# A fused attention and two-MoE kernel: the first block's output matmul in plain fp32, its weights split later, and a planner with other durations and due times

## The chip, the cores and the metric

The kernel runs on one core of a Trainium2 chip. The metric is the device time of one execution in microseconds. The core has a matrix engine (TensorE, PE in the rows), three engines for elementwise work (VectorE or DVE, ScalarE or ACT, GpSimd or POOL), and DMA queues, which SyncE (SP) issues. Each engine takes its instructions strictly in the order in which they were written; what couples the engines are semaphores.

## The reference

Three stages, each on the result of the one before, all float32:

```python
# attention: linear attention with decay, in chunks; x is [4, 8, 768, 32], B and C [4, 8, 768, 16]
    L = np.exp(cum[:, :, :, None] - cum[:, :, None, :]) * causal
    y = einsum(CB * L, xc) + einsum(Cc, state) * exp(cum)
    state = decay_full * state + sum(Bx)
# first MoE: 3072 tokens, d_model 256, d_ff 1536
    xn = x / rms * rms_g
    g = xn @ w_gate
    silu = g * (1.0 / (1.0 + np.exp(-g)))
    return silu * (xn @ w_val) @ w_out
# second MoE: d_ff 1024
    h = x @ w_in
    solu = h * softmax(h)
    return layernorm(solu) * g_ln @ w_out
```

## The kernel before

The 3072 tokens are 24 units of 128, in six blocks of four units. A unit goes through attention (`lpe`, `cb`, `mt`, `y`, `ms`, `rb`, `xn`, `xh`, `xl`: one matmul group for the decays and products, one for the result `y`, then the normalisation, which writes the split input of the first MoE). A block of 512 tokens goes through the first MoE in 12 steps of 128 hidden columns: a gate matmul group `g_gate` (six matmuls into `pg`), a value group `g_val` (six into `pv`), the activation (`g_tanh` on ACT, `g_silu` and `g_mul` on DVE), and the output `o_mm` (two halves, `po0` and `po1`, three matmuls each). Then a unit goes through the second MoE: `m_h` (12 matmuls into `ph`), the softmax on DVE and ACT, a transpose through DRAM (`m_tr`, `m_ds`, `m_dl`, tiles `dt`, `scr`, `tt`), a split of the result into `uth` and `utl` (`m_thd` on ACT, `m_tld` on DVE), and `m_f` (24 matmuls into `pf`). The last four units take a transpose on PE instead.

A float32 product at the fast rate needs split operands: a value is kept as a high part in the reduced type float32r and a low part, the difference, and a product is high x high, low x high and high x low, so three matmuls. The high part is a copy on ACT (`w_hi` for weights, `g_ah` for the activation), the low part a subtraction on DVE or GpSimd (`w_lo`, `g_al`). The weights of the MoEs come in as float64 bits of which DVE makes float32 in three instructions a piece (`w_conv`, lines 114, 117 and 120; 26 pieces of 512 columns: gate, value and output weights of the first MoE in turn, then those of the second). They are converted while the first two blocks run.

The order on every engine is made by a planner in the kernel (`plan`, line 994): `op(name, engine, duration, due, ...)` lists the operations with what they come after, which buffers they take (`new`) and use, and the planner places them one by one, at each engine the one with the earliest due time among those that could start soonest. Durations and due times only set the order; on the chip the semaphores decide. `alt` lets DVE work go to GpSimd. Due times come from constants: `PRO`, `FIRST` and `per1, perA, per2` give the start of each block, `Y0`, `YPOS`, `YSPAN` the attention, `HLAG` and `TAILGAP` the second MoE, `WGAP` and `wdue` the weights.

In what follows block, step and unit count from 0: unit 14's `ph` is the fifteenth group of 12 matmuls on line 473, its `pf` the fifteenth group of 24 on line 602.

Of the kernel before, what the change touches and what calls it, by code (L numbers as in the profile page):

```python
# [26 lines left out]
LAG = 2  # L27
AHEAD = 4
PRO = 34.0
FIRST = 63.0  # L30
WARM = 7
Y0 = (9.0, 4.0)
YPOS, YSPAN = 0.65, 1.0
TAILGAP = 5.0
SLACK = 0.1
SLACK0 = 0.1
VALATE = 5.0
EARLY = (-1.0, 1.5, 4.0, 6.0)
NPE = 4
MARGIN = {"PE": 0.5}  # L40
CROW = 30.0
WGAP = 8.0
HLAG = (50.0, 26.0)
# [3 lines left out]
        "xts": 2, "s2": 2, "ob": 1, "dt": 1, "scr": 2}  # L47
# [3 lines left out]
def fused_kernel(ctx, tc, aT, xbt, bcT, wg, wv, wo1, rg, wi2, wo2, gl, consts, out):  # L51
# [46 lines left out]
    wo2_s = wt([8, DM], "wo2")  # L98
# [24 lines left out]
    def w_f32(i):  # L123
        return wtm[i].bitcast(F32).rearrange("p (k f) -> p k f", k=2)
# [54 lines left out]
    def p_hi(c):  # L179
        A.activation(wo2_s[0][:, 4 * c:4 * c + 4], w2[c], AF.Copy)  # L180
# [434 lines left out]

    def g_mm(b, f, ws, tag):
# [87 lines left out]
    per1, perA, per2 = 12.4, 2.7, 6.5  # L704
# [44 lines left out]
    for u in range(NU):  # L749
        b, k = unit_blk[u]  # L750
        n = blk[b][1]
        if b == 0:
            Y = Y0[0] + Y0[1] * k
        else:
            Y = start[b - 1] + (k + YPOS) * (start[b] - start[b - 1]) / n * YSPAN
        s0 = u % 6 == 0
        if u >= SPLIT:
            op(f"lbc{u}", "SP", 1.6, Y - 14, (ld_bc4, u), new=[("bc", f"bc{u}")], kb=700)
# [44 lines left out]
        if u >= SPLIT:  # L803
            op(f"cb{u}", "PE", 0.5, Y - 12.0, (at_cbr, u), after=cbok + Lok[1], new=[("hc", f"pcb{u}")],
# [5 lines left out]
        op(f"y{u}", "PE", (1.4 if not s0 else 1.1) + (1.05 if yc else 0.0), Y, (at_ycb if yc else at_y, u),  # L810
# [24 lines left out]
    for b in range(NB):  # L835
# [3 lines left out]
        for f in range(NF):  # L839
# [12 lines left out]
            op(f"mu{s}", "DVE", v_us(N), t, (g_mul, b, f), after=[f"si{s}", f"vm{s}"], use=[f"th{s}", f"pv{s}"])  # L852
# [5 lines left out]
            for m in range(2):  # L858
                op(f"o{m}{s}", "PE", mm_us(N, 3), to, (o_mm, b, f, m), after=[f"al{s}"] + wo_n + ([f"o{m}{b}.{f-1}"] if f else []) + ([f"o0{s}"] if m else []),
# [18 lines left out]
    for u in range(NU):  # L878
# [12 lines left out]
        if not tl:  # L891
            op(f"h{u}.1", "PE", mm_us(512, 12), H, (m_h2, u), after=x2ok + win, new=[("hc", f"ph{u}")],
# [101 lines left out]
    def plan():  # L994
# [48 lines left out]
        while len(order) < len(ops):  # L1043
# [20 lines left out]
            if e != o["e"]:  # L1064
                o = ops[nm] = dict(o, us=o["alt"][0], fn=o["alt"][1])
# [116 lines left out]
```

## Time and profile before

| | us |
|---|---|
| Median of 3 runs | 558.02 (557.35 to 560.51) |
| The profiled execution | 554.45 |
| Its span, first to last instruction | 552.6 |
| PE busy | 524.9 (95%) |
| DVE busy | 422.8 (77%) |
| ACT busy | 309.5 (56%) |
| GpSimd busy | 117.7 (21%) |

The profile has the time of each instruction, what ended the idle time ahead of it, and the clock that PE was granted, as a share of 2.4 GHz. A busy time is the union of an engine's instructions; matmuls overlap each other in the pipeline, so that PE can be busy all the time and still not be at its peak. The rows of PE show an fp32 matmul as two records. "Critical" in the headings below is the chain of work that ended last, followed back from the last instruction.

### The profile page before, as it was taken

To read this page: it belongs to the slowest core of one execution; us is meant where nothing else is said; L and a number is where in the kernel's file an instruction comes from. 1 tells how busy PE (TensorE), PEld (TensorE's weight loads), DVE (VectorE), ACT (ScalarE), POOL (GpSimd) and SP (SyncE) were. 2 spreads that over 40 slices of the span, in tenths; PEclk is the share of its full clock that TensorE was granted. 3 is DMA by queue.
4 is the path that set the end of the run, shared out by engine and by line. 5 is a ranking of instruction groups with operands and counts; after the bars stand their busy time and mean duration, and the time that the engine had idled before them with its cause. 6 is when DMAs were issued, how large, how long until landed. Compare 5 with 4: busy or idle time off the path is not lost.

```text
span 552.6 us, 9279 instructions
## 1 busy us (share of the span) xinstructions
PE 524.9 (95%) x3240; PEld 438.2 (79%) x3240; DVE 422.8 (77%) x802; ACT 309.5 (56%) x670; POOL 117.7 (21%) x140
## 2 busy tenths in 40 slices
PE   8869998999999999999999999999999799999886
PEld 8847876777788888888888878878888688887786
DVE  4887999999996898778887878877875565375674
ACT  6526655565675675566674665765643343344455
POOL 1522443550320120424112212013302000010000
PEclk9868999999999999999999999999999899999999
DMA  5664755561174252363353264242221221022200
GB/s 169 182 194 148 232 186 187 180 191 57 46 219 144 86 178 91 105 185 108 104 167 105 80 184 134 92 148 93 56 86 49 77 79 55 11 76 87 85 21 28
DMA packets 44014, 65.00 MB, mean 118 GB/s; under 512 B 7360, under 2 KB 30272, under 8 KB 43968
## 3 DMA queue, kind: packets, MB, share of 16 engines
q1 hardware_dynamic: 43968, 64.42, 37.2%
q8 instruction: 25, 0.41, 0.3%
q14 instruction: 21, 0.17, 0.1%
HBM read 50.57 MB, written 13.83 MB: 117 GB/s over the span
## 4 chain that ended last, share of the span: by engine, by line
PE 64%; DVE 20%; DMA 7%; issue 4%; ACT 3%; SPq 2%; POOL 0%; DVEq 0%; ACTq 0%; POOLq 0%
PE pv L622 12%; PE pg L622 12%; PE po L664 11%; PE pf L602 11%; PE ph L473 10%; DMA xb<-in_xbt_dram 3%; DVE wt L117 3%; DVE wt L120 2%; DMA tt<-scr 2%; DVE th L644 2%; DVE th L640 2%; DVE al L656 2%; PE y L363 2%; DVE utl L578 2%; PE y L358 1%
## 5 line engine op out<-in xcount | busy, mean ns | idle before, releaser
L650 ACT ACTIVATE ah<-th 128x512 fp32r<-128x512 f32 x72 | 45.3, 629 | 61.9 <-PE po L664 38.2
L656 DVE TENSOR_TENSOR al<-th,ah 128x512 fp32r<-128x512 f32 x61 | 45.2, 740 | 25.7 <-ACT ah L650 25.4
L640 DVE SCALAR_TENSOR_TENSOR th<-th,pg 128x512 f32<-128x512 f32 x72 | 49.2, 684 | 18.5 <-ACT th L636 17.9
L622 PE MATMUL pg<-xh,wg_h 128*128 128x512 f32 x144 | 60.7, 421 | 2.7 <-DVE th L640 1.3
L664 PE MATMUL po<-ah,wo_h 128*128 128x512 f32 x144 | 58.9, 409 | 0.0
L664 PE MATMUL po<-al,wo_h 128*128 128x512 f32 x144 | 56.7, 393 | 2.2 <-DVE al L656 2.2
L622 PE MATMUL pv<-xh,wv_h 128*128 128x512 f32 x144 | 58.4, 406 | 0.2 <-DVE th L644 0.2
L622 PE MATMUL pg<-xl,wg_h 128*128 128x512 f32 x144 | 57.4, 399 | 0.4 <-DVE xl L442 0.4
L622 PE MATMUL pg<-xh,wg_l 128*128 128x512 f32 x144 | 57.0, 396 | 0.0
L622 PE MATMUL pv<-xl,wv_h 128*128 128x512 f32 x144 | 56.8, 394 | 0.0
L622 PE MATMUL pv<-xh,wv_l 128*128 128x512 f32 x144 | 56.8, 394 | 0.0
L664 PE MATMUL po<-ah,wo_l 128*128 128x512 f32 x144 | 56.7, 394 | 0.0
L602 PE MATMUL pf<-wo_h,utl 128*128 128x256 f32 x176 | 50.8, 289 | 5.4 <-DVE utl L578 5.4
L644 DVE TENSOR_TENSOR th<-pv,th 128x512 f32<-128x512 f32 x72 | 49.7, 690 | 7.0 <-PE pv L622 1.2
L602 PE MATMUL pf<-wo_h,uth 128*128 128x256 f32 x176 | 50.3, 286 | 4.1 <-ACT uth L573 4.1
L227 ACT ACTIVATE L<-L,cneg 128x128 f32<-128x128 f32 x160 | 50.5, 390 | 5.3 <-DMA L<-crow 5.1
L636 ACT ACTIVATE th<-pg 128x512 f32<-128x512 f32 x72 | 42.6, 592 | 17.8 <-PE pg L622 17.3
L602 PE MATMUL pf<-wo_l,uth 128*128 128x256 f32 x176 | 50.2, 285 | 0.0
L538 POOL TENSOR_TENSOR sc<-sc,mhalf 128x1 f32<-128x1 f32 x24 | 13.5, 564 | 169.3 <-DVE sc L533 165.2
L602 PEld LDWEIGHTS pf<-wo_h,utl 128*128 128x128 f32 x176 | 34.4, 195 | 7.4 <-DVE utl L578 6.7
L602 PEld LDWEIGHTS pf<-wo_h,uth 128*128 128x128 f32 x176 | 33.9, 192 | 5.7 <-ACT uth L573 5.0
L473 PE MATMUL ph<-wi_h,xh 128*128 128x512 f32 x96 | 37.9, 395 | 0.2 <-DVE L L298 0.2
(151 smaller groups left out, 1225.8 us busy)
## 6 DMA issues: line engine op xcount, KB each, us to landing
L<-crow SPq DMA_DIRECT2D x20, 512.0 KB
scr<-dt SPq DMA_DIRECT2D x20, 512.0 KB
tt<-scr SPq DMA_DIRECT2D x80, 128.0 KB
bc<-in_bcT_dram SPq DMA_DIRECT2D x48, 128.0 KB
stage<-in_wo_dram SPq DMA_DIRECT2D x10, 512.0 KB
xb<-in_xbt_dram SPq DMA_DIRECT2D x24, 192.0 KB
stage<-in_wg_dram SPq DMA_DIRECT2D x6, 512.0 KB
stage<-in_wv_dram SPq DMA_DIRECT2D x6, 512.0 KB
```

The costliest lines, as they stand in the source:

```text
L117: V.scalar_tensor_tensor(out=t, in0=v[:, :, 1], scalar=-0x40000000, in1=t, op0=ALU.bitwise_and, op1=ALU.bitwise_or)
L227: A.activation(d["L"][:, h], d["L"][:, h], AF.Exp, bias=cneg[:, u * 8 + h:u * 8 + h + 1])
L473: T.matmul(ph[c], xx[:, kk, k * P:(k + 1) * P], ww[:, kk, 512 * c:512 * c + 512], start=(i == 0), stop=(i == 5))
L538: G.tensor_tensor(out=sc[:, 7:8], in0=sc[:, 6:7], in1=mhalf, op=ALU.pow)
L602: T.matmul(d["pf"][:, 0:DM], uu[:, k], ww[:, k], start=(k == 0 and i == 0), stop=(k == 7 and i == 2))
L622: T.matmul(ps[:, :n], ww[:, kk, f * P:(f + 1) * P], xx[:, kk, :n], start=(i == 0), stop=(i == 5))
L636: A.activation(d["th"], d["pg"], AF.Tanh, scale=0.5)
L640: V.scalar_tensor_tensor(out=d["th"], in0=d["th"], scalar=1.0, in1=d["pg"], op0=ALU.add, op1=ALU.mult)
L644: V.tensor_tensor(out=d["th"], in0=d["pv"], in1=d["th"], op=ALU.mult)
L650: A.activation(d["ah"], d["th"], AF.Copy)
L656: e.tensor_tensor(out=d["al"], in0=d["th"], in1=d["ah"].bitcast(F32), op=ALU.subtract)
L664: T.matmul(po[b, m][:, :n], ww[:, f, m * P:(m + 1) * P], aa, start=(f == 0 and i == 0), stop=(f == NF - 1 and i == 2))
```

## The change

In block 0 the output matmul takes its operands unsplit, one plain fp32 matmul for each half of a step. `g_mul` writes its result into a buffer `aw`, in the storage of `ah` and `al` by turns, and `o_mm` multiplies it with the raw float32 weights, which the last conversion instruction now writes into a buffer `wraw` of their own (in the storage that the second MoE's `wo2` takes later). `g_ah` and `g_al` fall away in block 0. The split of the output weights, `w_hi` and `w_lo`, gets a due time 8 us ahead of block 1's use, and `w_lo` comes after the fp32 matmuls on the same piece. Besides, the planner's constants and durations have new values, and each block's attention and second MoE get an offset of their own (`YO`, `HO`).

```diff
-PRO = 34.0
-FIRST = 63.0
+PRO = 39.6
+FIRST = 61.0
...
-HLAG = (50.0, 26.0)
+HLAG = (52.3, 20.9)
+YO = (2.4, 2.27, 0.0, 2.59, -2.9)
+HO = (9.9, 2.75, 0.0, 0.0, -10.0, -6.6)
...
+    def w_raw(i):
+        c = pieces[i][0][1]
+        while len(wraw) <= c // 4:
+            nm = f"wo2_{'hl'[len(wraw)]}"
+            wraw.append(wp.tile([P, 4, 512], I32, name="wraw", tag=nm, bufs=1))
+        return wraw[c // 4][:, c % 4]
...
-            V.scalar_tensor_tensor(out=t, in0=v[:, :, 0], scalar=29, in1=t, op0=ALU.logical_shift_right,
+            raw = w_raw(i) if pieces[i][0][0] == "o" else t
+            V.scalar_tensor_tensor(out=raw, in0=v[:, :, 0], scalar=29, in1=t, op0=ALU.logical_shift_right,
                                    op1=ALU.bitwise_or)
...
     def g_mul(b, f):
         d = act[b, f]
-        V.tensor_tensor(out=d["th"], in0=d["pv"], in1=d["th"], op=ALU.mult)
+        out = d["th"]
+        if b < WIDE:
+            out = d["aw"] = sp.tile([P, NMAX], F32, name="aw", tag=awtag(f), bufs=BUFS[awtag(f)])[:, :blk[b][1] * P]
+        V.tensor_tensor(out=out, in0=d["pv"], in1=d["th"], op=ALU.mult)
...
-        for i, (aa, ww) in enumerate(((d["ah"], wo1_s[0]), (d["al"], wo1_s[0]), (d["ah"], wo1_s[1]))):
+        if b < WIDE:
+            T.matmul(po[b, m][:, :n], w_raw(3 * (f // 2) + 2).bitcast(F32)[:, 256 * (f % 2) + m * P:256 * (f % 2) + (m + 1) * P], d["aw"], start=f == 0,
+                     stop=f == NF - 1)
+        for i, (aa, ww) in enumerate(() if b < WIDE else ((d["ah"], wo1_s[0]), (d["al"], wo1_s[0]), (d["ah"], wo1_s[1]))):
...
-        op(f"wl{i}", "SP", 0.45, EARLY[i] if i < len(EARLY) else t - 6, (w_load, i), after=[f"wl{i-1}"] if i else [], new=[("u", f"st{i}")], kb=512)
+        op(f"wl{i}", "SP", 0.45, EARLY[i] if i < len(EARLY) else t - LEAD, (w_load, i), after=[f"wl{i-1}"] if i else [], new=[("u", f"st{i}")], kb=512)
...
+        if kind == "o":
+            t = gdue(WIDE, 2 * c + LAG) - 8.0
+            wu = [f"raw{c // 4}"]
...
+            last = [f"o{m}{b}.{2 * c + q}" for b in range(WIDE) for q in range(2) for m in range(2)]
...
-        op(f"w{i}", "DVE", 0.68, t, (w_lo, i, V), after=[f"wh{i}"], use=[f"wt{i}"], lock=True)
+        op(f"w{i}", "DVE", 0.68, t, (w_lo, i, V), after=[f"wh{i}"] + last, use=wu, lock=True)
...
+        H += HO[b]
```

`LEAD` is -2.11, and `WIDE` is 1.

What the change makes of the order is seen best at three places. The first is DVE in block 0, at step 0. Before, from the conversion of the second piece of gate weights (`L114` to `L120` into `wt`), with the activation of step 0 (`L640`, `L644`) and the low part `al`:

```order
L114 TENSOR_SCALAR wt<-stage 128x512
L640 SCALAR_TENSOR_TENSOR th<-th,pg 128x512
L644 TENSOR_TENSOR th<-pv,th 128x512
L117 SCALAR_TENSOR_TENSOR wt<-stage,wt 128x512
L120 SCALAR_TENSOR_TENSOR wt<-stage,wt 128x512
L656 TENSOR_TENSOR al<-th,ah 128x512
```

Now, at the same step (`L662` and `L669` are the activation, `L128` to `L135` the conversion):

```order
L135 SCALAR_TENSOR_TENSOR wraw<-stage,wt 128x512
L662 SCALAR_TENSOR_TENSOR th<-th,pg 128x512
L669 TENSOR_TENSOR aw<-pv,th 128x512
L128 TENSOR_SCALAR wt<-stage 128x512
L131 SCALAR_TENSOR_TENSOR wt<-stage,wt 128x512
L135 SCALAR_TENSOR_TENSOR wt<-stage,wt 128x512
```

The low part is gone, and the conversion of an output weight piece, into `wraw`, now ends right ahead of the activation of step 0.

The second place is PE at the passage from block 4 to block 5, where unit 14's `pf` begins. Before, ahead of it stand the last transpose of the attention (`y`) and the last output step of block 4 (two halves):

```order
L420 MATMUL y<-ident,r 128x128
L664 MATMUL po_4132<-ah,wo_h 128x512
L664 MATMUL po_4132<-al,wo_h 128x512
L664 MATMUL po_4132<-ah,wo_l 128x512
L664 MATMUL po_4144<-ah,wo_h 128x512
L664 MATMUL po_4144<-al,wo_h 128x512
L664 MATMUL po_4144<-ah,wo_l 128x512
L602 MATMUL pf<-wo_h,uth 128x256
L602 MATMUL pf<-wo_h,utl 128x256
L602 MATMUL pf<-wo_l,uth 128x256
```

Now, ahead of it stands the gate matmul of block 5, step 1:

```order
L644 MATMUL pg<-xh,wg_h 128x512
L644 MATMUL pg<-xl,wg_h 128x512
L644 MATMUL pg<-xh,wg_l 128x512
L621 MATMUL pf<-wo_h,uth 128x256
L621 MATMUL pf<-wo_h,utl 128x256
L621 MATMUL pf<-wo_l,uth 128x256
```

The same `pf` has moved behind the end of block 4's `ph` groups and into block 5. From unit 14's `ph` to it, PE's order has, now, the output step 7 of block 4, gate and value of step 10, output steps 8 and 9, gate and value of step 11, unit 15's `ph`, gate and value of block 5's step 0, output step 10 and that gate.

The third place is PE behind the last output matmul of block 5. Before:

```order
L664 MATMUL po_4918<-ah,wo_h 128x512
L664 MATMUL po_4918<-al,wo_h 128x512
L664 MATMUL po_4918<-ah,wo_l 128x512
L602 MATMUL pf<-wo_h,uth 128x256
L602 MATMUL pf<-wo_h,utl 128x256
L602 MATMUL pf<-wo_l,uth 128x256
```

Now:

```order
L692 MATMUL po_4856<-ah,wo_h 128x512
L692 MATMUL po_4856<-al,wo_h 128x512
L692 MATMUL po_4856<-ah,wo_l 128x512
L492 MATMUL ph<-wi_h,xh 128x512
L492 MATMUL ph<-wi_h,xl 128x512
L492 MATMUL ph<-wi_l,xh 128x512
```

Unit 18's `pf` stood there and unit 20's `ph` stands there now; unit 18's `pf` has moved ahead of the last gate matmul. The last output step is now behind two others (steps 9, 10 and 11 in a row), and behind it come the `ph` of units 20 and 21, then unit 19's `pf`.

## Rows read from the trace of the kernel before

**Rows 1.** Windows, by stage: stretch, length, engines' busy time (instructions), clock, DMA share, GB/s.

```profile
38.20:107.00 68.80, 65.55 (x411) 51.36 (x411) 62.69 (x116) 39.52 (x99) 25.21 (x26) 0.96 0.60 190
107.00:185.10 78.10, 75.45 (x467) 61.25 (x467) 70.88 (x126) 48.64 (x110) 20.76 (x23) 1.00 0.41 129
185.10:432.00 246.90, 245.82 (x1494) 206.28 (x1493) 189.98 (x358) 148.42 (x311) 52.08 (x59) 1.00 0.37 117
432.00:441.00 9.00, 5.89 (x30) 5.18 (x29) 6.58 (x14) 4.74 (x9) 0.55 (x1) 0.81 0.15 59
...
509.40:552.60 43.20, 33.39 (x227) 29.91 (x225) 25.71 (x68) 22.59 (x46) 2.71 (x5) 1.00 0.13 43
```

**Rows 2.** Critical chain, block 2: start, duration, engine and line, count.

```profile
243.87 1.39 PE pg L622 x6
```

**Rows 3.** Timeline of PE, start of the program: start, duration, instruction.

```profile
7.55 0.49 PE L978 MATMUL pd<-la,um 128*128 128x192 f32 x2
7.88 1.05 PE L269 MATMUL po<-um,la 128*128 128x128 f32 x8
8.86 1.16 PE L291 MATMUL pcb<-bc 16*128 16x128 f32 x16
```

**Rows 4.** Groups by line and shape, block 0: count, busy, mean ns, idle before.

```profile
L622 PE MATMUL pg<-xh,wg_h 128*128 128x512 f32 x25 | 11.3, 451 | 2.0 <-ACT xh L438 1.2 <-DVE th L640 0.8
...
L664 PE MATMUL po<-al,wo_h 128*128 128x512 f32 x22 | 8.7, 397 | 2.2 <-DVE al L656 2.2
...
L656 DVE TENSOR_TENSOR al<-th,ah 128x512 fp32r<-128x512 f32 x10 | 7.1, 712 | 0.3 <-ACT ah L650 0.3
```

**Rows 5.** Timeline in block 0, where PE waits for a low part.

```profile
94.44 1.59 DVE L120 SCALAR_TENSOR_TENSOR wt<-stage,wt 128x512 int32<-128x512 int32 x1
...
96.94 0.50 PE L664 MATMUL po<-al,wo_h 128*128 128x512 f32 x1 [2.24 <-DVE al L656]
```

**Rows 6.** Timeline ahead of block 0: DVE, a conversion and unit 2's state.

```profile
27.24 1.00 DVE L120 SCALAR_TENSOR_TENSOR wt<-stage,wt 128x512 int32<-128x512 int32 x1
...
28.68 0.27 DVE L379 SCALAR_TENSOR_TENSOR s<-s,e,y 128x64 f32<-128x64 f32 x1
```

**Rows 7.** Critical chain: `ph` and `pf` of unit 6, `ph` of units 14 and 18.

```profile
251.37 2.72 PE ph L473 x12
...
272.88 2.82 PE pf L602 x24
...
417.47 2.75 PE ph L473 x12
...
493.44 2.72 PE ph L473 x12
```

**Rows 8.** Timeline of the passage from block 4 to block 5.

```profile
432.44 0.40 PE L664 MATMUL po<-ah,wo_l 128*128 128x512 f32 x1
...
433.91 1.22 DVE L507 SCALAR_TENSOR_TENSOR ut<-ph,ut 128x1024 f32<-128x1024 f32 x1 [0.20 <-ACT ut L497]
...
434.88 0.38 PE L602 MATMUL pf<-wo_h,uth 128*128 128x256 f32 x1 [2.03 <-ACT uth L573]
...
435.06 1.22 DVE L578 TENSOR_TENSOR utl<-tt,uth 128x1024 fp32r<-128x1024 f32 x1
...
436.33 0.38 PE L602 MATMUL pf<-wo_h,utl 128*128 128x256 f32 x1 [1.08 <-DVE utl L578]
```

**Rows 9.** Timeline of the tail.

```profile
509.40 0.60 ACT L673 ACTIVATE xh<-po 128x512 fp32r<-128x512 f32 x1 [4.17 <-PE po L664]
...
512.16 0.38 PE L602 MATMUL pf<-wo_h,uth 128*128 128x256 f32 x1 [2.10 <-ACT uth L573]
...
513.62 0.38 PE L602 MATMUL pf<-wo_h,utl 128*128 128x256 f32 x1 [1.08 <-DVE utl L578]
...
527.23 0.39 PE L602 MATMUL pf<-wo_h,utl 128*128 128x256 f32 x1 [2.34 <-DVE utl L578]
```

**Rows 10.** Critical chain, the first load of weights.

```profile
2.18 5.49 DMA stage<-in_wg_dram
```

More of the change, by code (lines that the diff above doesn't have):

```diff
@@ L27 @@
 LAG = 2
+LEAD = -2.11
+PER = (12.7, 1.3, 6.5)
+WIDE = 1
 AHEAD = 4
-PRO = 34.0
-FIRST = 63.0
+PRO = 39.6
+FIRST = 61.0
 WARM = 7
[L32 to L36, printed above, removed]
+Y0 = (12.7, 2.9)
+YPOS = 0.58
+YSPAN = 0.84
+TAILGAP = 8.9
+SLACK = 0.19
+SLACK0 = 0.18
 VALATE = 5.0
-EARLY = (-1.0, 1.5, 4.0, 6.0)
+EARLY = (-1.0, -2.46, 4.0, 6.0)
 NPE = 4
 MARGIN = {"PE": 0.5}
-CROW = 30.0
-WGAP = 8.0
-HLAG = (50.0, 26.0)
+CROW = 37.3
+WGAP = 11.0
+HLAG = (52.3, 20.9)
+YO = (2.4, 2.27, 0.0, 2.59, -2.9)
+HO = (9.9, 2.75, 0.0, 0.0, -10.0, -6.6)
 TRACE = None
@@ L179, in p_hi @@
     def p_hi(c):
+        if not wo2_s:
+            wo2_s.extend(wp.tile([P, 8, DM], F32R, name=f"wo2_{s}", bufs=1) for s in "hl")
         A.activation(wo2_s[0][:, 4 * c:4 * c + 4], w2[c], AF.Copy)
@@ L731, in fused_kernel @@
             continue
-        op(f"wh{i}", "ACT", 0.63, t, (w_hi, i), after=[f"wc{i}.2"], use=[f"wt{i}"])
-        op(f"w{i}", "DVE", 0.68, t, (w_lo, i, V), after=[f"wh{i}"], use=[f"wt{i}"], lock=True)
+        wu = [f"wt{i}"]
+        last = []
+        if kind == "o":
+            t = gdue(WIDE, 2 * c + LAG) - 8.0
+            wu = [f"raw{c // 4}"]
+            ops[f"wc{i}.2"]["new"] += [(f"wo2_{'hl'[c // 4]}", wu[0])] if c % 4 == 0 else []
+            ops[f"wc{i}.2"]["use"] += wu
+            last = [f"o{m}{b}.{2 * c + q}" for b in range(WIDE) for q in range(2) for m in range(2)]
+        op(f"wh{i}", "ACT", 0.63, t, (w_hi, i), after=[f"wc{i}.2"], use=wu)
+        op(f"w{i}", "DVE", 0.68, t, (w_lo, i, V), after=[f"wh{i}"] + last, use=wu, lock=True)
         alt(f"w{i}", p_us(512), (w_lo, i, G))
@@ L740, in fused_kernel @@
         op(f"psub{c}", "DVE", 1.22, t, (p_sub, c), after=["pmean"], use=["mean"], lock=True)
-        op(f"phi{c}", "ACT", 1.06, t, (p_hi, c), after=[f"psub{c}"], use=["w2h", "w2l"])
+        op(f"phi{c}", "ACT", 1.06, t, (p_hi, c), after=[f"psub{c}"], use=["w2h", "w2l"],
+           new=[] if c else [("wo2_h", "w2H"), ("wo2_l", "w2L")])
         op(f"plo{c}", "DVE", 1.22, t, (p_lo, c), after=[f"phi{c}"], use=["w2h", "w2l"], lock=True)
@@ L803, in fused_kernel @@
         if u >= SPLIT:
-            op(f"cb{u}", "PE", 0.5, Y - 12.0, (at_cbr, u), after=cbok + Lok[1], new=[("hc", f"pcb{u}")],
+            op(f"cb{u}", "PE", 0.48, Y - 12.0, (at_cbr, u), after=cbok + Lok[1], new=[("hc", f"pcb{u}")],
                use=[f"bh{u}", f"cb{u}", f"pcb{u}"])
@@ L851, in fused_kernel @@
             op(f"si{s}", "DVE", v_us(N), t, (g_silu, b, f), after=[f"th{s}"], use=[f"th{s}", f"pg{s}"])
-            op(f"mu{s}", "DVE", v_us(N), t, (g_mul, b, f), after=[f"si{s}", f"vm{s}"], use=[f"th{s}", f"pv{s}"])
+            wide = b < WIDE
+            op(f"mu{s}", "DVE", v_us(N), t, (g_mul, b, f), after=[f"si{s}", f"vm{s}"], new=[(awtag(f), f"aw{s}")] if wide else [],
+               use=[f"th{s}", f"pv{s}"] + ([f"aw{s}"] if wide else []))
+            for m in range(2) if wide else ():
+                op(f"o{m}{s}", "PE", mm_us(N, 4), to, (o_mm, b, f, m), after=[f"mu{s}", f"wc{3*(f//2)+2}.2"] + ([f"o{m}{b}.{f-1}"] if f else []) + ([f"o0{s}"] if m else []),
+                   new=[(f"po{m}", f"po{m}{b}")] if f == 0 else [], use=[f"aw{s}", f"po{m}{b}", f"raw{f // 8}"])
+            if wide:
+                continue
             op(f"ah{s}", "ACT", a_us(N, 0.02), t + 2, (g_ah, b, f), after=[f"mu{s}"], new=[("ah", f"ah{s}")],
@@ L891, in fused_kernel @@
         if not tl:
-            op(f"h{u}.1", "PE", mm_us(512, 12), H, (m_h2, u), after=x2ok + win, new=[("hc", f"ph{u}")],
+            op(f"h{u}.1", "PE", mm_us(512, 12) + 0.02, H, (m_h2, u), after=x2ok + win, new=[("hc", f"ph{u}")],
                use=[f"ph{u}", f"x2{b}"])
@@ L940, in fused_kernel @@
         if not tl:
-            op(f"f{u}.3", "PE", mm_us(DM, 24), H + 1, (m_f4, u), after=[f"tl{u}.1"] + wout, new=[(tt[0], f"pf{u}")],
+            op(f"f{u}.3", "PE", 24 * 0.118, H + 1, (m_f4, u), after=[f"tl{u}.1"] + wout, new=[(tt[0], f"pf{u}")],
                use=[f"pf{u}"] + ku)
         for c in range(4) if tl else ():
-            op(f"f{u}.{c}", "PE", mm_us(DM, 6), H + 1, (m_f, u, c), after=[f"tl{u}.{c//2}"] + (wout if c == 0 else [f"f{u}.{c-1}"]),
+            op(f"f{u}.{c}", "PE", 6 * 0.118, H + 1, (m_f, u, c), after=[f"tl{u}.{c//2}"] + (wout if c == 0 else [f"f{u}.{c-1}"]),
                new=[(tt[0], f"pf{u}")] if c == 0 else [], use=[f"pf{u}"] + ku)
-        op(f"out{u}", "ACT", 0.4, H + 2, (m_out, u), after=[f"f{u}.3", f"sp{u}"], new=[("ob", f"ob{u}")],
+        op(f"out{u}", "ACT", 0.47, H + 2, (m_out, u), after=[f"f{u}.3", f"sp{u}"], new=[("ob", f"ob{u}")],
            use=[f"pf{u}", f"ob{u}"])
```

41 lines of the change are left out of this document (23 added, 18 removed).

## The prediction

> **What bounds the kernel now.** I read the stage table first [rows 1], since the average of PE over the whole span hides where it stalls. The stages are cut at the first gate matmul of a block (38.2, 107.0, 185.1 us), around the passage from block 4 to block 5, and at the last output matmul of block 5. PE is busy in 245.8 of 246.9 us from 185.1 to 432.0: there it is the bound, and a faster DVE or ACT is worth nothing. DVE is the fullest engine in block 0 after PE (62.7 of 68.8 us) and in block 1 (70.9 of 78.1).
>
> A busy PE is not a working PE, because matmuls overlap. The work of one is its distance to the next: six 512-column matmuls on split operands take 1.39 us on the chain, so 0.232 each [rows 2]. The two stages with holes are 432.0 to 441.0 (PE 5.9 of 9.0 us) and the tail after 509.4 (33.4 of 43.2); their second sign is the granted clock, 0.81 in the first, and 0.96 in block 0 [rows 1]. Half of full rate is the 1.2 GHz level, so 0.81 over 9.0 us is 3.4 us at 1.2 GHz, which cost 1.7 us; 0.96 over 68.8 us is 5.5 us there, 2.75 us lost, right after the idle start of the program.
>
> **The fp32 output matmuls: a loss.** In block 0 each of the 24 halves of an output step (12 steps, two halves) had three split matmuls, 3 x 0.232 = 0.695 us. Now it is one plain fp32 matmul. None with 512 columns is in the trace; narrower ones are, at full clock, and each instruction shows as two records [rows 3]. With 192 columns the two records take 7.88 - 7.55 = 0.33 us, 0.165 each; with 128 columns eight take 8.86 - 7.88 = 0.98, 0.1225 each. At 2.4 GHz that is 396 and 294 cycles: two cycles a column, and 12 to 38 cycles on top. For 512 columns this makes 1,036 to 1,062 cycles, 0.43 to 0.44 us a record and 0.86 to 0.89 an instruction; scaling the 128-column row bluntly gives 0.98. I take 0.88, by the wider row, which is the nearer one. 24 x (0.88 - 0.695) = **+4.4 us**, between +4.0 and +6.8. PE waits on few things in block 0, so I hide none of it.
>
> The rows put an instruction at four cycles a column in two records. The Trainium skill (FP8 and Floating Point Precision, TensorE Precision Notes) says it as four passes through the array for true fp32; priced as four of the 0.232 us matmuls that would be 0.93 us and +5.6 us in place of +4.4, inside the bounds above. No run here shows which it is at 512 columns.
>
> **What it takes off block 0: a gain.** Gone are 12 ACT copies (`ah`) and 12 subtractions (`al`), of which DVE had 10 at 0.712 us within the block [rows 4]. It does not clear DVE of that much: counted in the new order, between the last `xl` of block 0 and its last `mul`, DVE has 10 low-part subtractions of weights where it had 7, because it does fewer before the block. With every kind of instruction at the mean of its group in the trace the list falls from 66.5 to 62.1 us. The price of the full DVE queue is one row: a conversion of 1.59 us stands ahead of `al`, and PE, with the first of six matmuls done, waits 2.24 us [rows 5]. In all, PE's work in block 0 is 211 matmuls of 512 columns (25, 24, 24 gate, 72 value, 66 output; [rows 4] has the first gate group and one output group) x 0.232 = 49.0 us and about 12 us of attention; with the 2.75 us of half clock that leaves 68.8 - 63.8 = 5 us of such waits. With 62 us of DVE work beside 66 of PE I expect two engines close to each other and so not all of it back: **-3**, between 0 and -5. ACT gets room and needs none. The split of the output weights moves later: three low parts on GpSimd, three on DVE, all ahead of block 1's output matmuls, each waiting for the fp32 matmul that still reads the raw piece. Behind such a wait on DVE stand the `silu` of block 1 and so PE's next gate matmul; block 1 stays the DVE-bound stage that it is (67.9 us listed, 68.9 before) and I change nothing there.
>
> **The start.** Before block 0 the chain runs over the four attention units. In unit 2 the state update on DVE stood behind a conversion of 1.00 us and a normalisation, from 27.24 to 28.68 [rows 6], and the next unit waited for it. The new order has 26.0 us of DVE work, at the same means, up to the last `xl` where it had 28.7. A part of the chain is latency between engines: **-1.5**, between 0 and -3.
>
> **The passage from block 4 to block 5.** A unit of the second MoE leaves PE after its `ph` matmuls, goes through softmax, a DRAM transpose and the split, and comes back for its `pf` matmuls. PE is in order: if the unit is late, everything waits. Unit 14's `ph` began at 417.5 and its `pf` at 434.9, 17.4 us later, with PE stopped ahead of it [rows 7, 8]: PE waited 2.03 us for `uth` and, one matmul on, 1.08 us for `utl`, which stood behind another unit's 1.22 us product on DVE. The holes with their pipeline gaps are 434.88 - 432.67 and 436.33 - 435.00, 3.5 us, and the clock fell right after. In the new order I count between the two, at 1.39 us for each gate, value or output step: `ph` 2.7, eleven steps 15.3, another `ph` 2.7, so 20.7 us. Unit 6, 21.5 us apart in before (251.4 to 272.9), did not stop PE [rows 7]. So **-3.5** and, if PE is not idle, no drop of the clock: **-1.7**.
>
> **The tail.** The same twice more: unit 18 waits 2.10 + 1.08 us up to 513.62 and unit 19 2.34 us up to 527.23 [rows 9]; unit 18 had left at 493.4, 18.7 us before [rows 7]. With gaps as above that is 3.6 and 2.5 us. In the new order unit 18's `pf` (2.8 us) stands before the last gate matmul, 20.7 us after its `ph`, and unit 19's behind two `ph` groups, 19.4 us after its own. What is late next: with no `pf` left to fill, PE idles from the last output matmul until the copy and split of the second half are done, about 0.4 to the start of the copy, 0.60 for it [rows 9] and 0.7 for the split, less the 0.23 of the last matmul: 1.5 us, an estimate. The last units' `ph`, transposes and `pf` alternate one by one, and I put 1.1 us more than now to waits for the last two splits. The first hole of 3.6 so leaves 1.5: **-2.1 - 2.5 + 1.1 = -3.5**, between -2 and -4.1. In the other units the same distance is 19.8 to 27 us in the new order, so the middle stays as it is.
>
> **Sum.** 4.4 - 3 - 1.5 - 3.5 - 1.7 - 3.5 = **-8.8 us**. The profiled execution took 554.45 us, with a span of 552.6; it becomes 545.6. Three runs of before have the median 558.02 (557.35 to 560.51), so the profiled one was 0.6% quick; the same 8.8 us off the median is **549.2**.
>
> **Rivals.** (1) More is had: block 0 loses all 5 us of its waits and the start 3, the fp32 costs 4.0: 4.0 - 5 - 3 - 5.2 - 4.1 = -13.3, 544.7. For it: DVE is the fuller engine in block 0 and loses 4.4 us there. Against: the list of DVE is still 62 us. (2) The front gains nothing: DVE still sets the pace, the fp32 is paid in full, only the late holes go: 4.4 + 0 + 0 - 5.2 - 2 = -2.8, 555.2; with fp32 at +6.8, 557.6. For it: block 1, where DVE stays as full, and every conversion is still there. (3) Slower: the weight loads get due times 8 us later (their due time minus -2.11 in place of 6). If SP then issues them behind the attention loads, a piece lands after DVE wants it; the first one shows how long a piece takes, 5.5 us from issue to landing [rows 10]. It decides where a stage buffer stands empty when DVE reaches its conversion: if each of the 20 pieces left after the start comes 0.9 us late, 18 us are lost, and 8.8 gained elsewhere leave +9, 567. Against: in the new order the loads stand among the same attention loads as before, within a few places, and the four stage buffers, not the due time, held them back. (4) The clock stays at 1.2 GHz longer because block 0 starts with the same idle and the first output matmuls come later: twice the 2.75 us that it cost in block 0, on top, would be 5.5, and the time 554.7. For it: the start is as sparse as before. Against: from the first gate on the steps stand as close.
>
> **How the numbers follow.** About 0.5% (2.8 us) is what a measurement of this kernel can tell from no change. Forecast 549.2, from 546 to 553: 0.52. Rival 1: 0.16. Rivals 2 and 4 together: 0.22, of which 0.08 end below 555.2 and 0.14 within. Rival 3: 0.10. Faster 0.76, the same 0.14, slower 0.10. The range from 543 to 557 takes in rivals 1, 2 and 4 but for the last of the fp32 bound, and leaves out rival 3 and a tenth besides.
>
> **What would show it.** The `po<-aw` group at 0.86 to 0.98 us an instruction, start to start; block 0 still near 69 us from first gate to first gate; 432 to 441 without a stop before a `pf` and without a drop of the clock; the last output step followed by `ph` within 1.5 to 2 us; the time from the last output matmul to the end near 36 us where it was 43. Wrong it would be if `pf` waits for `uth` or `utl` in blocks 2 to 4, where I count on none, or if DVE waits for a `stage` transfer.

## The result: 540.3 us, twice the gain that was forecast

| | before | after |
|---|---|---|
| Median (lowest to highest) | 557.98 (557.35 to 560.51) | 540.34 (540.23 to 540.67) |
| The profiled execution | 554.45 | 540.26 |
| Its span | 552.6 | 538.5 |

The ratio is 0.968, with a 95% interval of 0.965 to 0.971. The time was forecast at 549.2: the direction was right, the size was not. The medians lie 17.6 us apart where the sum said 8.8; the two profiled executions lie 14.2 apart. So two things are to be found: some 5.4 us of gain in the profile that the sum missed, and 3.4 us that the profiled execution of before did not show.

The engines of the kernel after, from its page (busy time, share of the span, instructions):

```profile
PE 522.0 (97%) x3216; PEld 430.5 (80%) x3216; DVE 423.4 (79%) x788; ACT 301.7 (56%) x658; POOL 111.7 (21%) x142
```

DVE is as busy as it was, and PE too; only the span is shorter. The stages, with the columns of [rows 1]: from the first gate of blocks 0, 1 and 2 on, then the first 7.8 us of block 5, where the passage now lies, and the last output matmul to the end:

```profile
37.90:104.30 66.40, 65.50 (x385) 46.51 (x385) 59.49 (x109) 34.72 (x92) 19.41 (x21) 0.96 0.60 195
104.30:173.60 69.30, 68.91 (x410) 53.65 (x409) 64.99 (x113) 42.70 (x98) 18.64 (x24) 1.00 0.40 129
173.60:424.20 250.60, 250.60 (x1544) 212.48 (x1544) 202.74 (x368) 152.14 (x319) 54.80 (x66) 1.00 0.38 120
424.20:432.00 7.80, 7.80 (x45) 6.81 (x44) 6.70 (x11) 4.41 (x7) 1.29 (x1) 1.00 0.00 0
501.80:538.50 36.70, 30.44 (x202) 26.70 (x200) 21.12 (x59) 18.26 (x40) 2.20 (x4) 0.99 0.09 29
```

From block 1 to the passage PE has hardly a hole (68.91 of 69.30 us busy in block 1, then all of 250.60 and 7.80), and the clock is full. All waits of PE that the profile lists in blocks 0 and 1, and from 424 us to the end (what waited, for what: us in total, times, the longest):

```profile
PE pg L644 <- ACT xh L457: 1.2, 1, 1.2
PE y L417 <- ACT xts L445: 0.9, 1, 0.9
PE pg L644 <- DVE th L662: 0.2, 1, 0.2
...
PE pf L621 <- DVE xl L611: 1.7, 2, 1.3
PE pf L621 <- DVE utl L611: 1.0, 1, 1.0
PE ph L492 <- DVE xl L705: 0.2, 1, 0.2
```

The 2.24 us wait for `al` [rows 5] and the stops ahead of the `pf` of units 14, 18 and 19 [rows 8, 9] are gone; what is left late are waits of the last four units. The chain that ended last is PE for 78% of the span.

**Where the time went.** A stage holds other work in the two orders, so its length tells little. The table takes from the length of each stage, cut at the first gate matmul of each block, the matmuls in it at their full-rate distance (0.229 us for 512 columns, 0.118 for 256, 0.88 for an fp32 one of 512, narrower ones by their columns), and gives what is over against the kernel after, in us: stops, and what half clock costs. "Work" is the PE work itself. The lower rows are the experiments. Every row is one profiled execution: that of `e_old_due` was the slowest of its ten (553.76 against a median of 551.43), that of `e_old_h` the quickest of its four (546.70 against 549.49).

| | start | block 0 | 1 | 2 | 3 | 4 | 5 and tail | work |
|---|---|---|---|---|---|---|---|---|
| before | 0.3 | 4.9 | 2.6 | 0.0 | 0.8 | 7.0 | 3.1 | -4.6 |
| e_before | -0.2 | 4.9 | 2.4 | 0.0 | 0.5 | 6.1 | 7.8 | -4.6 |
| e_new_h | -0.8 | 5.6 | 1.6 | 0.4 | 0.1 | 0.4 | 1.4 | -4.6 |
| e_fp32_only | -0.1 | 5.1 | 1.7 | 0.2 | 0.3 | 6.6 | 6.9 | 0 |
| e_wide0 | -1.3 | 5.8 | -0.3 | 3.4 | 0.0 | 0.0 | -0.3 | -4.6 |
| e_old_dur | -0.9 | 3.6 | 3.5 | 0.4 | -0.1 | 0.0 | 1.9 | 0 |
| e_old_due | 2.6 | -0.8 | 1.0 | 1.3 | 0.8 | 1.7 | 6.9 | 0 |
| e_old_h | -0.9 | -0.2 | 0.0 | 0.2 | 0.3 | 2.0 | 5.0 | 0 |
| e_lead6 | 0.1 | -0.8 | 2.1 | 0.0 | -0.1 | 0.0 | 0.0 | 0 |
| e_dve10 | 0.1 | 6.7 | -0.2 | 0.0 | 0.0 | 0.0 | 0.0 | 0 |

The first row is the whole change: 18.7 us of stops and half clock taken away, 4.6 us of matmuls added, 14.1 in all.

### The profile page after: what moved, and what is told of

Its sections match the earlier page's. It is cut to its first block, busy times and chain, and to the rows that moved or that the text cites. A ratio compares the mean times of both kernels' runs of the same rounds, so it can differ in the third digit from the quotient of the medians.

```text
span 538.5 us, 9206 instructions
## 1 busy us (share of the span) xinstructions
PE 522.0 (97%) x3216; PEld 430.5 (80%) x3216; DVE 423.4 (79%) x788; ACT 301.7 (56%) x658; POOL 111.7 (21%) x142
## 4 chain that ended last, share of the span: by engine, by line
PE 78%; DVE 12%; ACT 3%; DMA 2%; issue 2%; SPq 2%; POOL 0%; DVEq 0%; ACTq 0%; POOLq 0%
PE pg L644 16%; PE pv L644 15%; PE po L692 14%; PE pf L621 12%; PE ph L492 11%; PE po L689 2%; PE y L382 2%; DVE wt L131 2%; PE y L377 1%; DVE th L662 1%; PE pcb L362 1%; PE pcb L310 1%; DVE wt L128 1%; DMA stage<-in_wg_dram 1%; PE y L417 1%
## 5 line engine op out<-in xcount | busy, mean ns | idle before, releaser
L644 PE MATMUL pg<-xh,wg_h 128*128 128x512 f32 x144 | 63.0, 438 | 1.4 <-ACT xh L457 1.2
L675 ACT ACTIVATE ah<-th 128x512 fp32r<-128x512 f32 x60 | 37.7, 628 | 46.8 <-PE po L692 29.5
L662 DVE SCALAR_TENSOR_TENSOR th<-th,pg 128x512 f32<-128x512 f32 x72 | 49.0, 681 | 11.5 <-ACT th L658 10.8
L644 PE MATMUL pv<-xh,wv_h 128*128 128x512 f32 x144 | 57.8, 401 | 0.0
L644 PE MATMUL pg<-xh,wg_l 128*128 128x512 f32 x144 | 57.1, 396 | 0.0
L644 PE MATMUL pg<-xl,wg_h 128*128 128x512 f32 x144 | 57.0, 396 | 0.0
L644 PE MATMUL pv<-xl,wv_h 128*128 128x512 f32 x144 | 56.6, 393 | 0.0
L644 PE MATMUL pv<-xh,wv_l 128*128 128x512 f32 x144 | 56.5, 392 | 0.0
L681 DVE TENSOR_TENSOR al<-th,ah 128x512 fp32r<-128x512 f32 x51 | 38.4, 753 | 18.6 <-ACT ah L675 18.6
L621 PE MATMUL pf<-wo_h,utl 128*128 128x256 f32 x176 | 49.5, 282 | 0.0
L692 PE MATMUL po<-ah,wo_h 128*128 128x512 f32 x120 | 48.9, 407 | 0.0
L692 PE MATMUL po<-al,wo_h 128*128 128x512 f32 x120 | 47.3, 394 | 0.0
L692 PE MATMUL po<-ah,wo_l 128*128 128x512 f32 x120 | 47.3, 394 | 0.0
L669 DVE TENSOR_TENSOR th<-pv,th 128x512 f32<-128x512 f32 x60 | 41.3, 689 | 7.0 <-PE pv L644 3.1
L516 ACT ACTIVATE ut<-ph,sc 128x1024 f32<-128x1024 f32 x20 | 22.3, 1114 | 30.4 <-DVE sc L503 30.4
L492 PE MATMUL ph<-wi_h,xl 128*128 128x512 f32 x96 | 37.5, 391 | 0.2 <-DVE xl L705 0.2
```

The lines of the kernel that those rows point to most:

```text
L492: T.matmul(ph[c], xx[:, kk, k * P:(k + 1) * P], ww[:, kk, 512 * c:512 * c + 512], start=(i == 0), stop=(i == 5))
L516: A.activation(d["u"], ph[0], AF.Exp, bias=sc[:, 0:1], accum_out=sc[:, 1:2])
L621: T.matmul(d["pf"][:, 0:DM], uu[:, k], ww[:, k], start=(k == 0 and i == 0), stop=(k == 7 and i == 2))
L662: V.scalar_tensor_tensor(out=d["th"], in0=d["th"], scalar=1.0, in1=d["pg"], op0=ALU.add, op1=ALU.mult)
L669: V.tensor_tensor(out=out, in0=d["pv"], in1=d["th"], op=ALU.mult)
L675: A.activation(d["ah"], d["th"], AF.Copy)
```

## The experiments

### The kernel before again, and the fp32 matmul alone

`e_before` is the kernel before, unchanged.

> The kernel before, once more and with its own profile. The first profiled execution of it took 554.45 us, the three others 557.35 to 560.51, so 3.6 us of the measured gain of 17.6 us may be no work at all but the execution that was profiled. If before simply varies from run to run, a second profile gives 554 to 560 us and the ratio is 1.00; where it is slower than 554.45, the comparison of the two profiles by stage shows where: a longer stretch at half clock, or longer waits in blocks 0 and 1. If the first profile was typical, this one shows 554 to 555 us.

Measured: 558.54 (553.11 to 560.98), ratio 0.999 (0.995 to 1.003). The median is no accident, and neither is the spread: 8 us, where four executions of the kernel after lie within 0.5. This profile, an execution of 557.08 us, shows what the one of before did not. Windows: the passage, the tail from the last output matmul, and two stretches of that tail:

```profile
430.90:439.90 9.00, 5.89 (x30) 5.15 (x29) 6.11 (x14) 4.85 (x9) 0.55 (x1) 0.81 0.15 59
508.10:555.40 47.30, 37.29 (x226) 33.77 (x224) 25.39 (x68) 22.33 (x46) 2.72 (x5) 0.89 0.12 40
...
511.20:518.00 6.80, 5.97 (x26) 5.77 (x27) 3.01 (x7) 1.72 (x3) 0.55 (x1) 0.50 0.19 77
528.20:531.60 3.40, 3.25 (x15) 3.25 (x16) 2.61 (x11) 0.61 (x2) 0.00 (x0) 0.50 0.02 5
```

The passage is that of [rows 1]: the same 9.0 us, 5.89 us of PE and clock of 0.81. The tail is 47.3 us from the last output matmul, where it was 43.0 (that matmul began at 509.66 us; the window in [rows 1] starts 0.26 earlier), at a clock of 0.89 where it was 1.00: 10.2 us at 1.2 GHz, right behind the waits of units 18 and 19, which cost half of that, 5.1 us. Of 51 executions of the kernel before that stand beside these runs, the 12 with a mean clock of 0.981 or more have a median span of 552.8 us, and the 23 at 0.973 or less 557.5. The profiled execution of before had 0.981, and its clock held through the tail; for most of the others only the mean clock is on record, and it is this one profile that shows where it falls.

`e_fp32_only` changes block 0 as the change does and leaves every due time, duration and planner rule old:

```diff
+WIDE = 1
...
+        if b < WIDE:
+            T.matmul(po[b, m][:, :n], w_raw(3 * (f // 2) + 2).bitcast(F32)[...], d["aw"], start=f == 0, stop=f == NF - 1)
```

> The changed kernel with every constant, duration and rule of the planner as before: only the plain fp32 output matmul of block 0 and the later split of its weights are left of the change. From block 1 on PE's order is that of before, with the same pf behind the last output steps of blocks 4 and 5. Theory A (the order brings the gain): fp32 costs 4.4 us on PE and gives back 3 in block 0, so 557 to 561 us, ratio 0.998 to 1.005. Theory B (the relief of VectorE brings it, the fp32 cost is hidden by waits that PE had in blocks 0 and 1): 550 to 554 us, ratio about 0.99.

Measured: 559.77 (556.22 to 563.66), ratio 1.004 (1.000 to 1.008). Alone it gains nothing, as theory A had it. Its first two blocks have about the stops of before by the table (5.1 and 1.7 against 4.9 and 2.6), and the added matmuls on top. Nor did DVE get room: in block 0, now 75.0 us, it is busy for 67.1, with 124 instructions where before had 116 [rows 1]; with the old numbers the planner put other work there (window of block 0):

```profile
37.80:112.80 75.00, 71.97 (x392) 48.86 (x393) 67.08 (x124) 35.44 (x94) 16.67 (x17) 0.94 0.58 189
```

### The order without the fp32 matmul

```diff
-WIDE = 1
+WIDE = 0
```

> The changed kernel with fp32 for no block: block 0 has its split operands, its copies and its subtractions again, everything else (constants, durations, raw weights in their own buffer) is as changed, and PE's order from block 3 on is that of the changed kernel. Theory A: the order keeps its gain, 540 to 546 us. Theory B: the front falls back, 548 to 553 us. By my prediction's own terms (fp32 +4.4, relief -3) it would be 1.4 us faster than the changed kernel, 539.

Measured: 544.24 (542.99 to 545.37), ratio 0.974 (0.968 to 0.980): inside theory A's range, above the 539 that the forecast's own terms gave. So the new order carries 14 us, and the fp32 matmul, although it adds 4.6 us of PE work, gains another 3.9. By the table its stops lie in block 0 (5.8 us) and block 2 (3.4). Behind the first gate the longest waits of PE up to the end of block 2 are all for DVE:

```profile
PE pg L644 <- DVE th L662: 3.2, 4, 1.0
PE po L692 <- DVE xl L705: 1.3, 1, 1.3
...
PE po L692 <- DVE al L681: 1.1, 2, 1.0
```

The low parts themselves (`al`) are the smallest of the three. The largest is the wait of the next gate for the `silu` (`th`), which stands behind other work on DVE. Why block 2 loses time, though the change touches only block 0's operands, was not traced.

### Is it the load of DVE, or the wait for the low part?

The kernel after, in its own order, with ten subtractions on DVE in block 0 whose result nobody reads. It puts the load of the low parts back, not the wait for them.

```diff
         V.tensor_tensor(out=out, in0=d["pv"], in1=d["th"], op=ALU.mult)
+        if b < WIDE and f % 6 != 5:
+            V.tensor_tensor(out=d["th"], in0=d["th"], in1=d["th"], op=ALU.subtract)
```

> The changed kernel in its own order, with a subtraction of 128x512 on DVE added right behind the product in ten of the twelve steps of block 0, of a value that nobody reads: it puts back the load that the low parts were for DVE (10 x 0.7 = 7 us), but not the wait of the output matmul for them. Theory (the fp32 output matmul gains by a shorter DVE queue): 543 to 547 us, with waits of PE for silu or gate operands in block 0. Rival (it gains because the output matmul no longer waits for copy and low part behind the product): 540 to 541.5 us.

Measured: 547.64 (544.08 to 549.94), 7.3 us more than the kernel after, a little above the theory's range and far from the rival's. Block 0 of the profiled execution, and what PE waited for in it behind the first gate:

```profile
38.10:111.10 73.00, 67.94 (x385) 46.05 (x385) 68.24 (x118) 34.06 (x92) 19.11 (x21) 0.96 0.55 179
...
PE y L417 <- ACT xts L445: 3.8, 2, 2.0
...
PE y L417 <- DVE s L398: 0.8, 1, 0.8
```

Eight of the ten instructions took 0.69 us, the others 1.59 and 1.26, so 8.4 us in all, and block 0 became 73.0 us where it was 66.4: 6.6 us more. So about four fifths of what is put on DVE here is passed on to the time. The waits are not those that the theory named: PE waits for nothing of the `silu`, but 3.8 us where it was 0.9 for the attention's `xts`, which ACT makes behind DVE's state update. In the kernel after DVE has little room in this block (59.5 of 66.4 us busy), and PE stops for little. That DVE's load is what the fp32 matmul relieves, `e_wide0` and this run show together; and it needs the new numbers, since in `e_fp32_only` DVE was about as full as before (89% against 91%) and the stops stayed.

### The due times of the second MoE, taken back and put in alone

`e_old_h` is the kernel after with the old lag and no offsets of the second MoE:

```diff
-HLAG = (52.3, 20.9)
+HLAG = (50.0, 26.0)
-HO = (9.9, 2.75, 0.0, 0.0, -10.0, -6.6)
+HO = (0.0, 0.0, 0.0, 0.0, 0.0, 0.0)
```

> The changed kernel with the second MoE's due times as before (HLAG old, all offsets HO zero); PE's order up to block 1 is that of the changed kernel but for the place of the first ph groups, and the tail has the order of before: unit 18's pf behind the last output step, then three ph groups. The prediction's terms for the tail say +3.5 us; the passage from block 4 to 5 is 0 to 3 us of that kind, since unit 14's pf stands some 20 us behind its ph here too. So 543 to 548 us. If instead the tail was not worth what I said, 540 to 542.

Measured: 549.49 (546.70 to 553.56), 9 us more than after, and the spread is back. The stops ahead of `pf` are back too (waits behind 495 us, and the window from 499 to the end, whose clock is 0.96):

```profile
PE pf L621 <- ACT uth L592: 3.5, 2, 2.5
PE pf L621 <- DVE utl L597: 2.0, 2, 1.1
...
499.00:545.00 46.00, 36.18 (x232) 32.25 (x230) 26.38 (x68) 22.40 (x46) 2.74 (x5) 0.96 0.12 41
```

`e_new_h` is the reverse, but for one constant: the kernel before with `HLAG`, `HO` and `TAILGAP` of the change and nothing else (`e_old_h` left `TAILGAP` new).

> The kernel before with only the due times of the second MoE new (HLAG, TAILGAP and the offsets HO); block 0 stays on split operands, all else is old. Theory: the stops ahead of pf at 432 and behind 509 us, and the half-clock stretches that follow them, are worth about 9 us by themselves, as in the reverse test: 547 to 551 us, no half-clock stretch after 45 us, and runs that agree within 2 us where those of the kernel before spread over 7. Rival: the new offsets fit only with the other new numbers, since the second MoE moves against blocks and attention that start elsewhere: stops remain, 554 to 560 us, spread as before.

Measured: 544.84 (544.27 to 546.88), ratio 0.981 (0.977 to 0.986), 12 us under the kernel before beside it (556.79), and below the theory's 547 to 551, with a spread of 2.6 us where 2 were expected; the rival falls. From 424 us on it waits over 0.2 us for two `pf` alone, of the last units; the window of its tail has the full clock:

```profile
PE pf L603 <- DVE utl L593: 2.0, 1, 2.0
PE pf L603 <- DVE xl L593: 1.0, 1, 1.0
...
500.00:542.60 42.60, 35.12 (x223) 30.45 (x221) 24.04 (x67) 20.82 (x44) 2.74 (x5) 1.00 0.13 42
```

So put in alone the due times of one stage bring 12 of the 17.6 us, and taken back they cost 9: half to two thirds of the gain. The two do not agree, since the parts of the change do not simply add. Another detail went against the expectation: one half-clock stretch, from 95.7 to 99.1 us, was left, behind the wait for `al` of [rows 5], which this kernel still has.

### Does the clock follow the holes?

The kernel before, in its own order and with its late steps as late as they were, but with matmuls in the holes whose results are thrown away: PE is busy, and nothing is done sooner.

```diff
         uh, ul = d["uT"]
+        for _ in range({14: 30, 18: 30, 19: 21}.get(u, 0) if c == 0 else 0):
+            T.matmul(d["pf"][:, 0:DM], wo2_s[0][:, 0, 0:P], wo2_s[0][:, 1], start=True, stop=True)
```

> The kernel before in its own order, with extra matmuls whose results are thrown away placed ahead of the pf of units 14 and 18 (30 of 256 columns each, 3.5 us) and 19 (21, 2.5 us), into the same pf bank. They lie in the holes in which PE waited for uth and utl (3.5, 3.6 and 2.5 us), so the step itself is not later than before. Theory (the half-clock stretches after 432 and 508 us come from these holes, and whether a tail has one or two of them is what spreads the runs of the kernel before over 553 to 563): no half clock from 45 us to the last 3 us, 552 to 554.5 us, a spread under 2.5 us. Rival (the clock falls for another reason, or only the first idle counts): 556 to 560, spread of 5 us or more.

Measured: 553.00 (552.48 to 554.06), ratio 0.990 (0.987 to 0.994); 5.8 us under the kernel before beside it, with a spread of 1.6 us. The filling ahead of unit 14's `pf`, the first `pf` matmul behind it, and the windows of passage and tail:

```profile
433.38 3.76 PE L601 MATMUL pf<-wo_h 128*128 128x256 f32 x30
436.98 0.28 PE L604 MATMUL pf<-wo_h,uth 128*128 128x256 f32 x1
...
431.90:441.00 9.10, 9.10 (x67) 8.66 (x66) 7.22 (x14) 5.15 (x9) 0.55 (x1) 1.00 0.15 59
509.00:551.90 42.90, 38.56 (x277) 35.86 (x275) 25.33 (x68) 22.23 (x46) 2.71 (x5) 0.99 0.13 44
```

From the start of the filling to the first `pf` there are 3.60 us, about the hole of 3.5 that it fills, and the clock is 1.00 where it was 0.81. So the clock has a price apart from the holes: 1.7 us behind the passage (half of 3.4 us), and of the 5.8 us on the median some 4 are then left for the tail, by difference. (The expectation held but for one stretch: 96.9 to 100.3 us was at half clock, behind the hole for `al` that was not filled.)

### Durations, due times, and the weight loads

`e_old_dur` is the kernel after with all durations and rules of the planner old, and the due constants new; `e_old_due` has the durations new, and all due constants old. Of each a line or two:

```diff
 e_old_dur
-            op(f"gm{s}", "PE", mm_us(N, 6) + 0.03, t, ...
+            op(f"gm{s}", "PE", mm_us(N, 6), t, ...
-                end[nm] = max(dma_free, t + o["us"] + 0.6) + 1.2
+                end[nm] = dma_free + 1.0
 e_old_due
-PRO = 39.6
+PRO = 34.0
-HLAG = (52.3, 20.9)
+HLAG = (50.0, 26.0)
...
```

> The changed kernel with the old durations and planner rules; the due constants and offsets are new, and block 0 is fp32. Theory (the due times carry the gain): 540 to 546 us, with at most two stops over 1 us ahead of a pf. Rival (the durations carry it): 552 to 560 us.

> The changed kernel with every due constant old (starts of blocks, attention, weights, second MoE) and the offsets at zero; the new durations and planner rules stay, and block 0 is fp32. Theory (the due times carry the gain): 553 to 560 us. Rival (the durations carry it, since the planner then places each step where it really fits): 540 to 547 us.

Measured: 547.66 (545.17 to 548.75) and 551.43 (548.75 to 553.76). Both miss the ranges of both theories: each half gives a part. What they lack stands in different stages. With the old durations blocks 0 and 1 have their stops back (3.6 and 3.5 us in the table) and the passage is clean; with the old due times blocks 0 and 1 have hardly any (-0.8 and 1.0), block 0 begins 2.6 us later, and the late stops are there (6.9). PE's waits of `e_old_dur` in blocks 0 and 1 and its windows of the two, then PE's waits of `e_old_due` behind 495 us:

```profile
PE pg L644 <- ACT xh L457: 2.1, 2, 1.2
PE pg L644 <- DVE th L662: 1.8, 2, 1.6
...
37.00:110.40 73.40, 70.64 (x392) 47.89 (x392) 68.48 (x123) 34.23 (x88) 21.03 (x20) 0.96 0.53 180
110.40:179.70 69.30, 65.21 (x400) 52.14 (x400) 59.63 (x109) 43.40 (x103) 13.78 (x16) 1.00 0.39 127
```

```profile
PE pf L621 <- DVE utl L597: 2.3, 1, 2.3
PE pf L621 <- ACT uth L592: 2.1, 1, 2.1
```

`e_lead6` sets the due time of the weight loads back.

```diff
-LEAD = -2.11
+LEAD = 6
```

> The changed kernel with the weight loads due 8.1 us earlier again (LEAD 6 in place of -2.11), all else as changed. Theory: four stage buffers and not the due time hold the loads back, so it matters little: 539 to 543 us. Rival (the later due time was part of the gain, since the weight loads then stand behind the attention loads on the load queue and these come in time): 545 us or more, with waits for attention loads in blocks 0 and 1. The other way (the later due time costs, the third rival of the prediction): under 538 us.

Measured: 541.65 (541.09 to 542.37), 1.3 us more than after. The range of the theory holds: the due time matters little. That it is the stage buffers which hold the loads back is the likely reason, and was not tested by itself. The little that is lost is in block 1 (2.1 us in the table, 0.8 won in block 0).

## Why the prediction was half of it

**The fp32 matmul (+4.4): right.** PE at the two halves of one output step, and the gate matmuls behind them:

```profile
61.68 1.88 PE L689 MATMUL po<-aw,wraw 128*128 128x512 f32 x4
63.00 0.80 PE L644 MATMUL pg<-xh,wg_h 128*128 128x512 f32 x1
63.63 0.40 PE L644 MATMUL pg<-xl,wg_h 128*128 128x512 f32 x1
```

From 61.68 to 63.63 two fp32 matmuls and one gate matmul of 0.23 took 1.95 us, so 0.86 each; over all 24 it is 0.89. That makes +4.0 to +4.7, about the forecast from the narrower rows [rows 3]. The Trainium skill (FP8 and Floating Point Precision, TensorE Precision Notes) puts true fp32 at four passes; the estimate from it, four of the 0.232 us matmuls or 0.93, is a little too much here.

**Block 0 (-3): too small.** 4.9 us went. The waits were counted at 5 us, and 2 of them were kept because two engines were "close to each other". That step failed: with the new numbers DVE's load and the time move together. `e_wide0`, with the low parts back, has 5.8 us more of stops in this block; `e_dve10` adds 8.4 us to DVE and 6.6 to the block. So the 4.4 us off the list were worth all of the waits and not a part. This is rival 1's term. Some 0.7 of the 4.9 us is clock and not DVE: the half-clock stretch of the start reached 6.2 us into block 0 and now reaches 4.8.

**Block 1 (nothing): wrong.** 2.6 us went. The step was that DVE's list stays as long, so the block stays as it is. DVE is even fuller than before, 65.0 of 69.3 us (94%) against 70.9 of 78.1 (91%) [rows 1], and PE waits for hardly any of it. `e_old_dur` is the counterpart: in its block 1 DVE has only 59.6 of 69.3 us (86%), and the stops are back, three of them in the first 6.5 us, for `xh` (0.86), `xl` (1.48) and `th` (1.64). Ahead of the last stands, on DVE, a conversion that itself waited for a weight transfer (`e_old_dur`, timeline):

```profile
113.82 0.89 DVE L128 TENSOR_SCALAR wt<-stage 128x512 int32<-128x512 int32 x1 [1.45 <-DMA stage<-in_wi_dram]
...
116.90 0.50 PE L644 MATMUL pg<-xh,wg_h 128*128 128x512 f32 x1 [1.64 <-DVE th L662]
```

So the fill of DVE does not tell here whether PE waits; what stands on DVE ahead of the step that PE wants does, a late transfer included. The planner's durations and rules, that of the DMA among them, set that order; which single one does it was not tried.

**The start (-1.5): wrong.** Block 0 began at 37.9 us, 0.3 sooner. The shorter list hardly shortened the chain, which still runs through conversions (chain of after; start, duration):

```profile
28.69 0.20 DVE s L398
...
31.43 0.60 DVE wt L131
...
37.45 0.43 ACT xh L457
...
37.92 2.96 PE pg L644 x6
```

Unit 2's state stands on this chain at 28.69 and on that of before at 28.76 (its timeline has 28.68 [rows 6]), and the first gate still waits 1.2 us for `xh`. The step took work off a queue and not off the path.

**The passage (-3.5 and -1.7): right, a little small.** Unit 14's `pf` follows its `ph` after 20.7 us (408.93 to 429.66), as counted, and without a stop:

```profile
408.93 0.40 PE L492 MATMUL ph<-wi_h,xh 128*128 128x512 f32 x1
...
429.43 0.39 PE L644 MATMUL pg<-xh,wg_l 128*128 128x512 f32 x1
429.66 0.28 PE L621 MATMUL pf<-wo_h,uth 128*128 128x256 f32 x1
429.78 0.28 PE L621 MATMUL pf<-wo_h,utl 128*128 128x256 f32 x1
```

(PE's timeline.) Block 4 loses 7.0 us less than before, 1.8 more than the two terms; 0.55 of that is a stop that before had at the block's first gate, the rest was not traced.

**The tail (-3.5): right in the profile.** 3.1 us with block 5; 36.7 us from the last output matmul to the end where 36 were forecast and 43.0 were before. Two parts missed and in part cancelled, which is luck: `ph` came 0.38 us behind the last output matmul and not 1.5 to 2, and the waits of the last units for their splits, 1.7 and 1.0 us in the list above, are 1.7 longer than before's, where 1.1 was put there. Before's, from 509 us on:

```profile
PE pf L602 <- DVE xl L592: 1.0, 1, 1.0
```

**From the profile to the median: the step that cost most.** "The same 8.8 us off the median" took the 3.6 us between the profiled execution and the median as a common offset. They were half clock in the tail, behind the very holes that the change closes, so they went too. `e_before` shows the half clock; `e_fill`, which fills the holes and does nothing sooner, takes it away, together with the 1.7 us of the passage. The sign stood in the numbers given: a spread of 3 us and a profiled execution quicker than all three runs.

**The rivals.** Rival 1 had the right direction and the right block, at 544.7; that it came nearest is in part luck, since it has 3 us from the start, which did not come, and lacks the 3.4 us of the median. Rival 2 (the front gains nothing) fell: blocks 0 and 1 gave 7.5 us. Rival 3 (the weight loads) is refuted by `e_lead6`: with the old due time the kernel is 1.3 us slower and not quicker; and of the stage transfers DVE in the kernel after waited only for the first, at the start of the program (1.7 us, 1.9 before). Rival 4 did not come: block 0's clock is 0.96, as it was.

In sum, profile against profile: fp32 +4.6 (4.4 forecast), start -0.3 (-1.5), blocks 0 and 1 -7.5 (-3), block 3 -0.8 (0), block 4 with the passage -7.0 (-5.2), block 5 and tail -3.1 (-3.5), together -14.1; and some 3.4 more that the profiled execution of before did not have to lose.

## What to carry to other kernels

Before a difference is moved from a profiled execution to a median, ask why the two differ: where the runs of a kernel spread by a per cent, look at the granted clock of each, and at the holes behind which it falls, since closing such a hole gains its length and the half clock behind it. In a stage where two engines are nearly full, as in block 0 here, work taken off the one that the other waits for can be worth about all its time, but only if the order lets what the other waits for come first; a queue's total does not tell that. A step taken off a queue but not off the path gains next to nothing, as the start showed.

## What the runs showed of the hardware

The same hole is followed by half clock in some executions and not in others. The tail of before and of `e_before`, one and the same kernel, is the first case: behind the same waits of units 18 and 19 its clock was 1.00 in one execution and 0.89 in the other. The second is in block 0: the wait of 2.24 us for `al` stands in the kernel before and in `e_fill` at the same place of the order; the window behind it, in `e_fill` and then in before:

```profile
96.90:100.30 3.40, 3.40 (x25) 2.73 (x27) 3.33 (x7) 0.16 (x1) 0.00 (x0) 0.50 0.00 0
```

```profile
96.90:100.30 3.40, 3.36 (x47) 2.93 (x49) 3.33 (x6) 0.00 (x0) 0.00 (x0) 1.00 0.00 0
```

And a part of an fp32 matmul's time shows behind its records: the four records of two such matmuls stand within 1.32 us (61.68 to 63.00), and the gate matmul behind them is 0.63 us from the next where others are 0.23. Whoever prices an fp32 matmul by the starts of its records alone finds 0.66 us and not 0.86.
